# A planned one-core kernel: new costs for its planner, and 64-bit weights rounded by an integer add

## The chip, the cores and the metric

The kernel runs on one NeuronCore of a Trainium2 chip. The metric is the device time of one execution in microseconds (us). The engines are TensorE (matmuls; PE in the profile, PEld its weight loads), VectorE (DVE), ScalarE (ACT), GpSimd (POOL) and SyncE (SP), which issues nearly all DMAs. Each engine works through its own queue in order.

## The reference, cut to what matters

Three stages follow each other: a linear attention with a delta rule over 768 tokens (4 batches, 8 heads of 48), a dense block with a squared ReLU, and a dense block with a maximum over three products.

```python
for t in range(S):                                   # S = 768
    y[:, :, t] = einsum('bhd,bhde->bhe', q[:, :, t], state)
    v_old = einsum('bhde,bhd->bhe', state, kt)       # kt: k over its norm
    state = state + bt * einsum('bhd,bhe->bhde', kt, vt - v_old)
x = y.transpose(0, 2, 1, 3).reshape(B * S, H * D)    # 3072 x 384
r = maximum(x @ w_in, 0); x = (r * r) @ w_out        # 384 x 2048, 2048 x 384
h = maximum(maximum(x @ w1, x @ w2), x @ w3)         # 384 x 768 each
out = h @ w_out2                                     # 768 x 384
```

The weights arrive as 64-bit floats; the other inputs are float32.

## The kernel before, in words

The tokens are cut into 6 steps of 128 positions, each over all 4 batches (512 columns). For each step `gram` forms the products of keys with keys and queries (64x64 matmuls of `W`), `solve` inverts a triangular system of 32x32 blocks on VectorE (31 pairs of instructions, `tmp<-L,T` and `T<-T,tmp`, each needing the one before it) and finishes with 32x32 matmuls, and `chain` runs the recurrence over two chunks of 64 tokens with small matmuls (64x48 and 48x64). These matmuls are float32, and I call them small. A small matmul stands twice in the trace, each time with a weight load; a 128x128 transpose stands once.

`moe1(t)` is the first dense block of step t: 16 blocks f of 128 hidden columns; `hidden` makes 9 matmuls (three parts of x, each as high times high, high times low, low times high) and `project` 9 more. These are fp32r matmuls with 512 columns, called large here. In `moe1(0)` the blocks f = 0 to 7 run in two halves of 256 columns, so that the first half of step 0's tokens can start early. Between the two, ScalarE makes `r` and `gh`, VectorE makes `gl`. The second dense block (tiles `b0` to `b3`, `m0`, `m1`) comes last and is large matmuls alone.

`load_w` brings one 128x384 block of weights: a DMA into `raw`, ScalarE's absolute value, six VectorE instructions (a seventh, the low part, comes after ScalarE's `hi`), so that `hi + lo` is the weight rounded to float32. There are 32 loads for the first block, all inside `moe1(0)`, and 24 for the second, much later.

The order on every engine is written by the class `Planner`: all operations are recorded, each with a due place (`pl.at`, from tables such as `GRAM`, `SOLVE`, `CHAIN`) and a cost from `_Engine.record`. `forward` then plays the engines against these costs and picks, at each free engine, the ready operation with the earliest due place; on TensorE it prefers to stay with small or with large matmuls by the rules `MIX`, `FULL`, `STAY`, `BURST`, `URGENT`. `backward` sets the due places anew, and the best of 8 rounds is issued.

Of the kernel before, what the change touches and what calls it, by code (L numbers as in the profile page):

```python
# [52 lines left out]
class Planner:  # L53
# [3 lines left out]

    MIX, FULL, STAY, BURST, URGENT = 3719.33, 7024.00, 12.67, 2.43, 3.70  # L60
    INTO, BACK, RUSH = 0.09, 0.2, 0.52
    HOLD = {"vector": 0.071}
    LAG = {"tensor": 0.2, "vector": 0.13, "scalar": 0.15, "gpsimd": 0.08, "sync": 0.0}

    def __init__(self, nc):
        self.nc, self.at, self.ops, self.seen, self.joint, self.beside = nc, 0.0, [], {}, None, False
        self.free, self.first, self.end, self.before_all, self.rush = {}, 0, {}, False, False
        self.flow, self.ticks, self.start = (deque(), False, False), {}, {}
# [7 lines left out]
        yield  # L76
        self.joint, self.beside = None, False

    def add(self, engine, call, cost, outs, ins, flow, late):
        if self.joint is None or self.joint == len(self.ops):  # L80
            self.ops.append([engine, [], 0.0, set(), self.at, any(a.dtype == F32R for a in ins), 0.0, 0.0, self.before_all, self.rush])
        n = len(self.ops) - 1
        op = self.ops[n]
        op[1].append(call)
        op[2] = max(op[2], cost) + 0.007 if self.beside else op[2] + cost
# [28 lines left out]
    def forward(self, at):  # L114

        first, ops = self.first, self.ops
        free, ticks, flow, fill, big = dict(self.free), dict(self.ticks), *self.flow
        flow = deque(flow)
        left, ready, queue, seq = {}, {}, {}, []
        start, end = {}, self.end  # L120
# [13 lines left out]
        todo = len(ops) - first  # L134
        while todo:
            best = None
            for e in set(ready) | set(queue):
# [46 lines left out]
            if e == "tensor":  # L184
# [13 lines left out]
            if e == "sync":  # L198
                free[e] = t + 0.6
                free["dma"] = max(t + 1.3, free.get("dma", 0.0)) + cost  # L200
                end[n] = free["dma"] + 1.0
            else:
                free[e] = end[n] = t + cost
                if e == "scalar":
                    end[n] += ops[n][7]
# [5 lines left out]
        return seq, start, end, (free, ticks, (flow, fill, big))  # L211

    def backward(self, end):

# [13 lines left out]
        todo = len(left)  # L228
        while todo:
            best = None  # L230
            for e in set(ready) | set(queue):
                f = free.get(e, 0.0)
                if queue.get(e):
                    t = f
# [48 lines left out]
class _Engine:  # L283
# [3 lines left out]
    def __getattr__(self, what):  # L287
        fn = getattr(getattr(self.plan.nc, self.name), what)

        def record(*args, **kw):  # L290
# [5 lines left out]
            cols, late = out.free_size(), 0.0  # L296
            space = ins[0].space if ins else None
            if self.name == "tensor":
                k, m = ins[0].partition_size(), ins[0].free_size()
                if ins[0].dtype == F32R:  # L300
                    cost = cols / 2400 + 0.015
                elif what == "transpose":
                    cost = 0.11
                else:
                    cost = max(1.67 * cols, 100) / 1000
                    if m <= 32:
                        cost = 0.027
                    elif out.offset >= _row(out.tensor):
                        cost = 0.007
            elif self.name == "vector":  # L310
                fast = what in ("tensor_scalar", "tensor_copy") and space != PSUM
                cost = (cols / (2 if fast else 1) + 64) / 960
                if what == "transpose":
                    cost = (cols * 1.8 + 64) / 960
                elif what == "reciprocal":
# [1 line left out]
            elif what == "dma_start" and self.name == "scalar":  # L317
                cost, late = 0.65, 2.0
            elif self.name == "scalar":
                cost = (cols + (60 if space == PSUM else 112)) / 1200  # L320
# [9 lines left out]
            self.plan.add(self.name, lambda: fn(*args, **kw), cost, [out], ins, flow, late)  # L330

        return record

# [2 lines left out]
def kernel(  # L336
# [41 lines left out]
    GB = B // 2  # L378
    EPS = 1e-6

    GL, CL, G1, DEC, BOOST, SPL, CUT, HALF, G2, LATE, BLOCKS, FIRST, HURRY = 27, 46, -1, 97, 164, 47, 6, 8, -133, 228, 3, 2, 0
    GRAM = (0, -8, 0, 23, 17, 0)
    SOLVE = (0, 0, 0, 80, 12, -33)
    CHAIN = (-9, -8, 0, 11, -5, -19)
    TICKS = 6 * NF
    W_MIN, W_MAX = 2.0 ** -15, 122876.0

# [435 lines left out]
    def load_w(src, hi, lo, like=None):  # L823


        raw, t1, t2 = raw_ring(), xs_ring()[:, 0:DM], t2_ring()
# [4 lines left out]
        u1, u2 = t1.bitcast(U32), t2.bitcast(U32)  # L831
        pl.scalar.activation(t1, high.bitcast(F32), AF.Abs)
        pl.vector.tensor_scalar(t1, t1, W_MIN, W_MAX, op0=ALU.max, op1=ALU.min)
        pl.vector.tensor_scalar(
            u1, u1, 3, 0x3FFFFFFF, op0=ALU.logical_shift_left, op1=ALU.bitwise_and
        )
        pl.vector.scalar_tensor_tensor(
            u1, high, 0xC0000000, u1, op0=ALU.bitwise_and, op1=ALU.bitwise_or
        )
        pl.vector.tensor_scalar(u2, u1, 0xFF800000, None, op0=ALU.bitwise_and)  # L840
        pl.vector.scalar_tensor_tensor(t2, low, 2.0 ** -52, t2, op0=ALU.mult, op1=ALU.mult)
        pl.vector.tensor_tensor(t1, t1, t2, op=ALU.add)
        if like is not None:
            t1 = like(t1)
        pl.scalar.activation(hi, t1, AF.Copy)
        pl.vector.tensor_tensor(lo, t1, hi.bitcast(F32), op=sub)

    def load_in(src, f, hi, lo):
        sv = src.rearrange("(r p) f -> p r f", p=P)
# [8 lines left out]
    def moe1(t, first=0, last=NF):  # L858
# [63 lines left out]
        pl.at = at + 6 * NF + 3 - BOOST  # L922
        if t + 1 < NS:
            for o in range(KD):
                xs = xs_ring() if t + 2 < NS else x2r[1][:, o]
                if o == 1:
                    pl.vector.tensor_copy(xs, acc[o])
                else:
# [168 lines left out]
```

## Time and profile before

| | |
|---|---|
| median of 3 runs | 941.7 us (940.34 to 943.5) |
| the profiled execution | 943.03 us |
| its span in the profile | 940.6 us |
| PE busy | 868.4 us, 92% |
| DVE busy | 588.4 us, 63% |
| ACT busy | 443.1 us, 47% |

The span runs from the first to the last recorded instruction; the 2.4 us around it belong to the execution's own time. The shares are means over stages that have different limits, so the table alone does not say which engine sets the end.

### The profile page before, as it was taken

What the parts mean: (1) busy time and instruction counts of PE and PEld (TensorE: products, weight loads), DVE (VectorE), ACT (ScalarE), POOL (GpSimd) and SP (SyncE); (2) the same over time, 40 slices, a digit from 0 to 9 for tenths busy, and PEclk for the clock granted to TensorE, in tenths of its full rate; (3) what the DMA queues carried; (4) which work ended last, traced back from release to release, by engine and by line L of the source; (5) the groups of instructions that cost most, each with busy time, mean ns of one, the idle gap of its engine ahead of it and who ended that gap; (6) DMA issues with size and microseconds to landing.
All of it is one profiled execution on the core that took longest, in us unless ns stands there. A gap on an engine that the chain in (4) does not pass through costs nothing.

```text
span 940.6 us, 22413 instructions
## 1 busy us (share of the span) xinstructions
PE 868.4 (92%) x9388; PEld 731.2 (78%) x9388; DVE 588.4 (63%) x1256; ACT 443.1 (47%) x835; POOL 23.4 (2%) x33
## 2 busy tenths in 40 slices
PE   5537789999989998999999999999999999999998
PEld 4426678877877777877887888888898989898987
DVE  4999998899858957955963399883313132323221
ACT  6446458965465464555456567662212122221121
POOL 2001001000000010010000000000000000000000
PEclk9555799999999999999999999999999999999999
DMA  9744467677744746333432567670010100000000
GB/s 170 146 118 123 107 178 226 160 180 180 176 94 93 194 98 109 113 121 72 132 102 85 179 193 238 190 225 1 1 68 1 68 1 34 0 34 1 26 9 34
DMA packets 186276, 100.64 MB, mean 107 GB/s; under 512 B 150080, under 2 KB 166208, under 8 KB 186176
## 3 DMA queue, kind: packets, MB, share of 16 engines
q1 hardware_dynamic: 185328, 99.02, 40.5%
q8 instruction: 73, 1.20, 0.5%
q10 hardware_dynamic: 848, 0.20, 0.1%
q14 instruction: 27, 0.22, 0.1%
HBM read 79.53 MB, written 14.94 MB: 100 GB/s over the span
## 4 chain that ended last, share of the span: by engine, by line
PE 74%; DVE 14%; ACT 5%; DMA 3%; issue 3%; SPq 0%; DVEq 0%; ACTq 0%
PE ps L330 74%; DVE xs L330 3%; DVE T L330 2%; DVE tmp L330 2%; ACT G L330 2%; DVE t L330 2%; DVE W L330 1%; DMA raw<-in_moe_w_out_dram 1%; DMA raw<-in_moe_w_in_dram 1%; ACT r L330 1%; ACT W L330 1%; DVE gl L330 1%; ACT US L330 1%; DVE L L330 1%; ACT xs L330 0%
## 5 line engine op out<-in xcount | busy, mean ns | idle before, releaser
L330 DVE TENSOR_TENSOR r<-r,ps 128x512 f32<-128x512 f32 x72 | 49.5, 687 | 178.6 <-PE ps L330 176.6
L330 PE MATMUL ps<-gh,wo 128*128 128x512 f32 (+1 forms) x624 | 156.3, 379 | 2.8 <-ACT gh L330 2.0
L330 ACT ACTIVATE r<-ps 128x512 f32<-128x512 f32 (+1 forms) x140 | 79.9, 571 | 152.3 <-PE ps L330 142.9
L330 PEld LDWEIGHTS ps<-gh,wo 128*128 128x128 f32 x624 | 111.3, 189 | 25.2 <-ACT gh L330 2.4
L330 PE MATMUL ps<-xh,wih 128*128 128x512 f32 (+1 forms) x312 | 121.8, 390 | 2.2 <-ACT r L330 2.1
L330 PE MATMUL ps<-xh,wil 128*128 128x512 f32 (+1 forms) x312 | 117.8, 378 | 1.3 <-issue 0.9
L330 PE MATMUL ps<-xl,wih 128*128 128x512 f32 (+1 forms) x312 | 117.5, 377 | 0.0
L330 DVE TENSOR_TENSOR gl<-r,gh 128x512 fp32r<-128x512 f32 (+1 forms) x104 | 67.1, 646 | 47.2 <-ACT gh L330 45.0
L330 PE MATMUL ps<-gl,wo 128*128 128x512 f32 (+1 forms) x312 | 84.2, 378 | 2.3 <-DVE gl L330 1.3
L330 PEld LDWEIGHTS ps<-xh,wih 128*128 128x128 f32 x312 | 59.5, 191 | 15.3 <-ACT r L330 3.9
L330 PEld LDWEIGHTS ps<-xh,wil 128*128 128x128 f32 x312 | 59.7, 191 | 11.3 <-issue 1.3
L330 PEld LDWEIGHTS ps<-xl,wih 128*128 128x128 f32 x312 | 59.7, 191 | 10.6
L330 ACT ACTIVATE gh<-r 128x512 fp32r<-128x512 f32 (+1 forms) x104 | 62.1, 597 | 10.1 <-PE ps L330 7.8
L330 PEld LDWEIGHTS ps<-gl,wo 128*128 128x128 f32 x312 | 56.3, 189 | 13.5 <-DVE gl L330 1.7
L330 ACT ACTIVATE G<-ps 32x256 f32<-32x256 f32 (+3 forms) x132 | 55.4, 432 | 23.7 <-PE ps L330 21.6
L330 DVE TENSOR_TENSOR T<-T,tmp 128x31 f32<-128x31 f32 (+15 forms) x186 | 62.9, 338 | 3.5
L330 DVE TENSOR_TENSOR tmp<-L,T 128x31 f32<-128x31 f32 (+15 forms) x186 | 62.7, 337 | 3.3
L330 ACT ACTIVATE r<-r 128x512 f32<-128x512 f32 (+1 forms) x104 | 62.0, 596 | 2.4
L330 PE MATMUL ps<-W 64*64 64x64 f32 x1536 | 45.5, 246 | 14.1 <-ACT W L330 10.6
L330 PEld LDWEIGHTS ps<-W 64*64 64x64 f32 x1536 | 38.7, 156 | 21.1 <-ACT W L330 13.2
L330 DVE TENSOR_SCALAR xs<-xs 128x384 f32<-128x384 f32 x112 | 40.9, 366 | 15.0 <-ACT xs L330 14.2
L330 ACT ACTIVATE m0h<-r 128x512 fp32r<-128x512 f32 x18 | 11.4, 632 | 67.1 <-DVE r L330 67.1
(149 smaller groups left out, 1662.2 us busy)
## 6 DMA issues: line engine op xcount, KB each, us to landing
wo<-wod SPq DMA_DIRECT2D x88, 384.0 KB, 3.4
raw<-in_moe_w_out_dram SPq DMA_DIRECT2D x22, 384.0 KB, 3.6
raw<-in_moe_w_dram SPq DMA_DIRECT2D x18, 384.0 KB, 3.8
raw<-in_moe_w_in_dram SPq DMA_DIRECT2D x16, 384.0 KB, 4.2
wod<-wo SPq DMA_DIRECT2D x16, 384.0 KB, 3.7
vn<-in_v_dram SPq DMA_DIRECT2D x24, 192.0 KB, 4.4
kn<-in_k_dram SPq DMA_DIRECT2D x24, 192.0 KB, 4.8
out_dram<-ob SPq DMA_DIRECT2D x24, 192.0 KB, 1.9
```

The costliest lines, as they stand in the source:

```text
L330: self.plan.add(self.name, lambda: fn(*args, **kw), cost, [out], ins, flow, late)
```

## The change

There are three edits. First, `load_w` rounds in another way: the low word is scaled by 2^-29 on ScalarE, which leaves it as a small whole number in `raw`, and VectorE adds it as an integer to the float's bits. Two VectorE instructions fall away, the float add becomes an add on 16-bit halves (an instruction over 128x768 elements of two bytes, named `ISA` in the order below), and ScalarE has one instruction more. The tiles `xs` and `t2` give way to two `word` tiles and a third `raw` tile; the 12 stores of `x2d` go through `raw` tiles.

Second, the planner has other costs, and it counts TensorE's instructions: a boundary every 256 (`CHUNK`) may not come sooner than 3.6 us (`SUPPLY`) after the last, and when small matmuls are ahead of that by 128 (`AHEAD`), it turns to large ones. Third, all rules' numbers and due places are new; one line of each table is shown.

```diff
-    MIX, FULL, STAY, BURST, URGENT = 3719.33, 7024.00, 12.67, 2.43, 3.70
+    MIX, FULL, STAY, BURST, URGENT = 1297.88, 4709.68, 69.71, 12.05, -3.99
+    CHUNK, SUPPLY, AHEAD = 256, 3.6, 128
...
+                used = count % self.CHUNK - self.CHUNK * (t - since) / self.SUPPLY
+                thin = used > (0 if thin else self.AHEAD)
                 if None not in kinds:
-                    if fill:
+                    if fill or thin:
                         n = kinds[True][1]
...
+                over = (count + ops[n][10]) % self.CHUNK
+                if over < count % self.CHUNK:
+                    cost += max(0.0, since + self.SUPPLY - t - cost)
+                    since = t + cost
+                count += ops[n][10]
...
-    CHAIN = (-9, -8, 0, 11, -5, -19)
+    CHAIN = (-692, -620, 84, -317, 132, 232)
...
-    xs_ring = Ring(tiles(const, 2, [P, TB], F32, "xs"))
-    raw_ring = Ring(tiles(const, 2, [P, 2 * DM], U32, "raw"))
-    t2_ring = Ring(tiles(const, 2, [P, DM], F32, "t2"))
+    raw_ring = Ring(tiles(const, 3, [P, 2 * DM], U32, "raw"))
+    word_ring = Ring(tiles(const, 2, [P, DM], U32, "word"))
...
-        pl.scalar.activation(t1, high.bitcast(F32), AF.Abs)
-        pl.vector.tensor_scalar(t1, t1, W_MIN, W_MAX, op0=ALU.max, op1=ALU.min)
+        pl.scalar.activation(value, high.bitcast(F32), AF.Abs)
+        pl.vector.tensor_scalar(value, value, W_MIN, W_MAX, op0=ALU.max, op1=ALU.min)
+        pl.scalar.activation(low, low, AF.Copy, scale=2.0 ** -29)
         pl.vector.tensor_scalar(
-            u1, u1, 3, 0x3FFFFFFF, op0=ALU.logical_shift_left, op1=ALU.bitwise_and
+            word, word, 3, 0x3FFFFFFF, op0=ALU.logical_shift_left, op1=ALU.bitwise_and
         )
         pl.vector.scalar_tensor_tensor(
-            u1, high, 0xC0000000, u1, op0=ALU.bitwise_and, op1=ALU.bitwise_or
+            word, high, 0xC0000000, word, op0=ALU.bitwise_and, op1=ALU.bitwise_or
         )
-        pl.vector.tensor_scalar(u2, u1, 0xFF800000, None, op0=ALU.bitwise_and)
-        pl.vector.scalar_tensor_tensor(t2, low, 2.0 ** -52, t2, op0=ALU.mult, op1=ALU.mult)
-        pl.vector.tensor_tensor(t1, t1, t2, op=ALU.add)
+        pl.vector.tensor_tensor(word, word, low, op=ALU.add)
```

How the order moves is shown at two places. The first is VectorE in the first `solve` (step 0), at the middle of its 31 pairs. Before, the pairs (`tmp`, `T`) alternate with instructions of weight loads (`xs`, `t`, `wil`):

```order
L330 SCALAR_TENSOR_TENSOR t_85<-raw_83,t_85 128x384
L330 TENSOR_TENSOR tmp<-L,T 128x255
L330 TENSOR_TENSOR xs_81<-xs_81,t_85 128x384
L330 TENSOR_TENSOR T<-T,tmp 128x17x15
L330 SCALAR_TENSOR_TENSOR t_84<-raw_82,t_84 128x384
L330 TENSOR_TENSOR tmp<-L,T 128x256
L330 TENSOR_TENSOR wil<-xs_81,wih 128x3x128
L330 TENSOR_TENSOR T<-T,tmp 128x16x16
```

Now the same pairs stand alone there:

```order
L341 TENSOR_TENSOR tmp<-L,T 128x252
L341 TENSOR_TENSOR T<-T,tmp 128x18x14
L341 TENSOR_TENSOR tmp<-L,T 128x255
L341 TENSOR_TENSOR T<-T,tmp 128x17x15
L341 TENSOR_TENSOR tmp<-L,T 128x256
L341 TENSOR_TENSOR T<-T,tmp 128x16x16
L341 TENSOR_TENSOR tmp<-L,T 128x255
L341 TENSOR_TENSOR T<-T,tmp 128x15x17
```

The weight work that stood between the pairs has moved behind them; 22 pairs in a row, from the first, have nothing between them.

The second place is TensorE while `chain(2)` and `gram(3)` run inside `moe1(1)`, at the first chunk's update of the state (`US,kn`). `W` marks the small matmuls of `gram`, `gh,wo` and `xh,wih` large ones. Before:

```order
L330 MATMUL ps_90<-W_105 64x64
L330 MATMUL ps_88<-gh_77,wo_99 128x512 x2
L330 MATMUL ps_93<-R,G_108 64x48 x16
L330 MATMUL ps_92<-US_109,kn 48x48 x16
L330 MATMUL ps_91<-W_105 64x64
L330 MATMUL ps_90<-W_105 64x64
L330 MATMUL ps_91<-W_105 64x64
```

And now:

```order
L341 MATMUL ps_89<-W_104 64x64
L341 MATMUL ps_92<-R,G_107 64x48 x16
L341 MATMUL ps_91<-US_108,kn 48x48 x16
L341 MATMUL ps_88<-xh,wih 128x512
L341 MATMUL ps_88<-xh,wil 128x512
L341 MATMUL ps_88<-xl,wih 128x512
L341 MATMUL ps_88<-xh,wih 128x512
L341 MATMUL ps_88<-xh,wil 128x512
L341 MATMUL ps_88<-xl,wih 128x512
L341 MATMUL ps_85<-gl_78,wo_97 128x512
L341 MATMUL ps_86<-gl_78,wo_97 128x512
```

Before, 80 small matmuls follow each other here, with 2 large ones ahead of them and 3 behind. Now 16 large ones stand behind the 64 small ones that end with `US,kn`, and 18 ahead of them.

## Rows read from the trace of the kernel before

**Rows 1.** The page: busy time of the engines, and the queue that brings TensorE's instructions.

```profile
PE 868.4 (92%) x9388; PEld 731.2 (78%) x9388; DVE 588.4 (63%) x1256; ACT 443.1 (47%) x835; POOL 23.4 (2%) x33
...
q8 instruction: 73, 1.20, 0.5%
```

**Rows 2.** Busy time in stretches: start and end, length, then each engine's us (instructions).

```profile
core 0: us, PE busy (x) PEld busy (x) DVE busy (x) ACT busy (x) POOL busy (x), PEclk, DMA share, GB/s
19.00:102.00 83.00, 42.50 (x946) 35.59 (x944) 79.58 (x206) 42.27 (x88) 2.85 (x3) 0.59 0.56 131
102.00:214.60 112.60, 105.50 (x1644) 91.72 (x1640) 105.82 (x263) 79.46 (x174) 5.19 (x7) 0.97 0.65 172
214.60:518.70 304.10, 291.59 (x4709) 236.70 (x4708) 216.44 (x439) 166.73 (x296) 10.45 (x11) 0.99 0.50 120
518.70:937.00 418.30, 418.29 (x1948) 358.77 (x1944) 179.09 (x328) 143.54 (x255) 0.00 (x0) 1.00 0.23 73
...
560.00:580.00 20.00, 20.00 (x90) 16.57 (x89) 19.13 (x42) 15.48 (x29) 0.00 (x0) 1.00 0.70 224
```

**Rows 3.** TensorE in order of time: start, length, what, and the wait before it.

```profile
102.07 0.58 PE L330 MATMUL ps<-xh,wih 128*128 128x256 f32 x1
...
214.63 0.92 PE L330 MATMUL ps<-US,kn 64*48 64x48 f32 x32
...
518.73 1.65 PE L330 MATMUL ps<-gh,wo 128*128 128x512 f32 x6
```

**Rows 4.** VectorE in order of time: three marks of the first stage.

```profile
21.76 1.93 DVE L330 STREAM_TRANSPOSE L<-G 128x1024 f32<-128x1024 f32 x1 [0.42 <-ACT G L330]
...
101.48 0.42 DVE L330 TENSOR_TENSOR xl<-xr,xh 128x256 fp32r<-128x256 f32 x1
...
213.81 0.69 DVE L330 TENSOR_TENSOR gl<-r,gh 128x512 fp32r<-128x512 f32 x1
```

**Rows 5.** Groups of instructions by shape: busy us in all, mean ns of one.

```profile
L330 DVE SCALAR_TENSOR_TENSOR t<-raw,t 128x384 f32<-128x384 uint32 x56 | 31.0, 553 | 0.7
L330 ACT ACTIVATE xs<-raw 128x384 f32<-128x384 f32 x56 | 30.9, 552 | 25.5 <-DMA raw<-in_moe_w_out_dram 7.3 <-DMA raw<-in_moe_w_in_dram 4.8 <-DMA raw<-in_moe_w_dram 4.3
L330 DVE TENSOR_TENSOR xs<-xs,t 128x384 f32<-128x384 f32 x56 | 30.8, 550 | 0.6
...
L330 DVE TENSOR_SCALAR t<-xs 128x384 uint32<-128x384 uint32 x56 | 20.4, 365 | 0.6
...
L330 DVE TENSOR_TENSOR vn<-vn,nn 128x768 f32<-128x768 f32 x12 | 11.4, 953 | 1.1 <-DMA vn<-in_v_dram 1.1
```

**Rows 6.** VectorE in order of time: independent neighbours, then a chain.

```profile
70.60 0.54 DVE L330 TENSOR_TENSOR wo<-xs,wo 128x384 fp32r<-128x384 f32 x1
71.07 0.26 DVE L330 TENSOR_TENSOR T<-T,tmp 128x112 f32<-128x112 f32 x1
...
157.16 0.75 DVE L330 TENSOR_SCALAR xs<-xs 128x384 f32<-128x384 f32 x2 [0.28 <-ACT xs L330]
157.94 0.56 DVE L330 SCALAR_TENSOR_TENSOR xs<-raw,xs 128x384 uint32<-128x384 uint32 x1
```

**Rows 7.** Busy time in stretches of 64 small matmuls of `solve`, and of 12 large ones.

```profile
491.85:493.07 1.22, 1.22 (x129) 1.18 (x129) 0.60 (x1) 1.11 (x2) 0.00 (x0) 1.00 0.70 186
258.71:260.66 1.95, 1.43 (x130) 1.27 (x129) 0.00 (x0) 1.48 (x2) 0.00 (x0) 1.00 0.43 131
...
493.07:496.01 2.94, 2.94 (x20) 2.17 (x12) 1.39 (x3) 2.74 (x5) 1.90 (x2) 1.00 0.16 62
```

**Rows 8.** PEld's waits at 256 to 292, 332 to 371, 411 to 450: total, times, longest.

```profile
PEld ps L330 <- issue: 4.7, 8, 1.2
...
PEld ps L330 <- issue: 6.7, 9, 2.1
...
PEld ps L330 <- issue: 5.2, 8, 1.3
```

**Rows 9.** DMA queues from 256 to 282: packets, MB, share.

```profile
q8 instruction: 7, 0.11, 2.0%
```

More of the change, by code (lines that the diff above doesn't have):

```diff
@@ L67, in __init__ @@
         self.free, self.first, self.end, self.before_all, self.rush = {}, 0, {}, False, False
-        self.flow, self.ticks, self.start = (deque(), False, False), {}, {}
+        self.flow, self.ticks, self.start = (deque(), False, False, (0, -9.0, False)), {}, {}
         for name in ("tensor", "vector", "scalar", "gpsimd", "sync"):
@@ L77, in together, with add @@
         self.joint, self.beside = None, False
-    def add(self, engine, call, cost, outs, ins, flow, late):
+    def add(self, engine, call, cost, outs, ins, flow, late, share=0.0, count=0):
         if self.joint is None or self.joint == len(self.ops):
-            self.ops.append([engine, [], 0.0, set(), self.at, any(a.dtype == F32R for a in ins), 0.0, 0.0, self.before_all, self.rush])
+            self.ops.append([engine, [], 0.0, set(), self.at, any(a.dtype == F32R for a in ins), 0.0, 0.0, self.before_all, self.rush, 0, 0.0, 0.0])
         n = len(self.ops) - 1
@@ L84, in add @@
         op[1].append(call)
-        op[2] = max(op[2], cost) + 0.007 if self.beside else op[2] + cost
+        op[10] += count
+        op[11], op[12] = max(op[11], cost), op[12] + share
+        op[2] = max(op[11], op[12]) if self.beside else op[2] + cost
         op[6] += flow
@@ L136, in forward @@
             best = None
-            for e in set(ready) | set(queue):
+            for e in self.LAG:
                 f = free.get(e, 0.0)
@@ L203, in forward @@
                 free[e] = end[n] = t + cost
-                if e == "scalar":
-                    end[n] += ops[n][7]
+                end[n] += ops[n][7]
             todo -= 1
@@ L210, in forward @@
                     there(m)
-        return seq, start, end, (free, ticks, (flow, fill, big))
+        return seq, start, end, (free, ticks, (flow, fill, big, (count, since, thin)))
     def backward(self, end):
@@ L230, in backward @@
             best = None
-            for e in set(ready) | set(queue):
+            for e in self.LAG:
                 f = free.get(e, 0.0)
@@ L295, in record @@
                 ins.append(out)
-            cols, late = out.free_size(), 0.0
+            cols, late, share, count = out.free_size(), 0.0, 0.0, 0
             space = ins[0].space if ins else None
@@ L299, in record @@
                 k, m = ins[0].partition_size(), ins[0].free_size()
+                count = 2
                 if ins[0].dtype == F32R:
-                    cost = cols / 2400 + 0.015
+                    cost = cols / 2400 + 0.0133
                 elif what == "transpose":
@@ L304, in record @@
                 else:
[L305 to L309, printed above, removed]
+                    count = 4
+                    cost = 1.7 * cols / 1000 if m > 32 else 0.027
+                    share = cols * (1.0 if k > 64 else 0.68 if k > 32 else 0.6) / 1000
             elif self.name == "vector":
@@ L312, in record @@
                 cost = (cols / (2 if fast else 1) + 64) / 960
+                if space == PSUM or len(ins) > 1 and ins[1].space == PSUM:
+                    cost, late = cost + 0.09, -0.09
                 if what == "transpose":
@@ L319, in record @@
             elif self.name == "scalar":
-                cost = (cols + (60 if space == PSUM else 112)) / 1200
+                cost = (cols + 180) / 1160 if space == PSUM else (cols + 124) / 1200
+                late = -0.11 if space == PSUM else 0.0
             elif self.name == "gpsimd":
@@ L329, in record @@
                 flow = k * cols / 128 * (1 if ins[0].dtype == F32R or what == "transpose" else 2)
-            self.plan.add(self.name, lambda: fn(*args, **kw), cost, [out], ins, flow, late)
+            self.plan.add(self.name, lambda: fn(*args, **kw), cost, [out], ins, flow, late, share, count)
         return record
@@ L823, in load_w @@
     def load_w(src, hi, lo, like=None):
-        raw, t1, t2 = raw_ring(), xs_ring()[:, 0:DM], t2_ring()
+        raw, word = raw_ring(), word_ring()
         pl.before_all = raw_ring.n <= FIRST
@@ L830, in load_w @@
         low, high = raw[:, 0:2 * DM:2], raw[:, 1:2 * DM:2]
-        u1, u2 = t1.bitcast(U32), t2.bitcast(U32)
-        pl.scalar.activation(t1, high.bitcast(F32), AF.Abs)
-        pl.vector.tensor_scalar(t1, t1, W_MIN, W_MAX, op0=ALU.max, op1=ALU.min)
+        value = word.bitcast(F32)
+        pl.scalar.activation(value, high.bitcast(F32), AF.Abs)
+        pl.vector.tensor_scalar(value, value, W_MIN, W_MAX, op0=ALU.max, op1=ALU.min)
+        pl.scalar.activation(low, low, AF.Copy, scale=2.0 ** -29)
         pl.vector.tensor_scalar(
-            u1, u1, 3, 0x3FFFFFFF, op0=ALU.logical_shift_left, op1=ALU.bitwise_and
+            word, word, 3, 0x3FFFFFFF, op0=ALU.logical_shift_left, op1=ALU.bitwise_and
         )
         pl.vector.scalar_tensor_tensor(
-            u1, high, 0xC0000000, u1, op0=ALU.bitwise_and, op1=ALU.bitwise_or
+            word, high, 0xC0000000, word, op0=ALU.bitwise_and, op1=ALU.bitwise_or
         )
-        pl.vector.tensor_scalar(u2, u1, 0xFF800000, None, op0=ALU.bitwise_and)
-        pl.vector.scalar_tensor_tensor(t2, low, 2.0 ** -52, t2, op0=ALU.mult, op1=ALU.mult)
-        pl.vector.tensor_tensor(t1, t1, t2, op=ALU.add)
+        pl.vector.tensor_tensor(word, word, low, op=ALU.add)
         if like is not None:
-            t1 = like(t1)
-        pl.scalar.activation(hi, t1, AF.Copy)
-        pl.vector.tensor_tensor(lo, t1, hi.bitcast(F32), op=sub)
+            value = like(value)
+        pl.scalar.activation(hi, value, AF.Copy)
+        pl.vector.tensor_tensor(lo, value, hi.bitcast(F32), op=sub)
     def load_in(src, f, hi, lo):
@@ L924, in moe1 @@
             for o in range(KD):
-                xs = xs_ring() if t + 2 < NS else x2r[1][:, o]
+                xs = raw_ring()[:, 0:TB].bitcast(F32) if t + 2 < NS else x2r[1][:, o]
                 if o == 1:
```

12 lines of the change are left out of this document (6 added, 6 removed).

## The prediction

> **What bounds the kernel now.** I read the busy time by stretches first. The reader is to see four stages there [rows 2]. [...] From 214.6 to 518.7 TensorE is busy 291.6 of 304.1 us and VectorE only 216. From 518.7 on TensorE is busy 418.29 of 418.30 us and everything else has room. So an end can come earlier only by what TensorE finishes sooner before 518.7.
>
> The marks between the stages come from the order of time [rows 3]. The first large matmul starts at 102.07. At 214.63 the 432nd is done: all 288 half-width ones of the first step and 144 of full width. At 518.73 the last small matmul is done, with 1332 large ones issued; I counted these places in the written order and found their rows. Behind that stand 1944 large matmuls without a gap. A full-width one costs 20/90 = 0.222 us [rows 2], in the last line.
>
> In the first two stages VectorE sets the pace. Its marks are the start of the first `solve` at 21.76, the first `xl` at 101.48, which the first large matmul needs, and the 24th `gl` at 213.81, the last of step 0, which stands at the same place as TensorE's 214.63 [rows 4].
>
> In the third stage the wait to look at is "issue", in which TensorE waits for nothing that the profile shows. The same 64 small matmuls of `solve` take 1.22 us in one place and 1.95 in another, where TensorE is busy for 1.43 only [rows 7]. The two engine rows hold 18,776 instructions, and the instruction queue brought 73 packets, so one packet serves 257 [rows 1]. From 256 to 282 us seven came, one in 3.7 us [rows 9]. A small matmul is four instructions (two records, each with a weight load), so 64 of them use up a packet in 1.22 us. A large one is two instructions in 0.222 us, a packet in 28 us. In dense stretches of small matmuls the instructions therefore come too slowly. In the three rounds where `gram` and `chain` meet, the weight loads wait 4.7, 6.7 and 5.2 us for "issue" [rows 8].
>
> **The weight loads.** Each load loses one `TENSOR_SCALAR` (0.365) and one `SCALAR_TENSOR_TENSOR` (0.553) on VectorE [rows 5], 0.92 us. The float add (0.550) becomes the 16-bit add, which the trace does not show. Its lower bound is 0.365, like a single-source instruction on as many words; its upper bound is 0.953, that of `vn`, which takes 768 elements one by one. I take 0.55: the instruction writes as many bytes as the float add, which is the nearest row. [...]
>
> ScalarE's extra instruction is like `xs<-raw`, 0.552 [rows 5]. It can run as soon as the absolute value is out, beside two `TENSOR_SCALAR` and a `SCALAR_TENSOR_TENSOR` of VectorE, so I cost it at nothing. If that cover went, VectorE would wait in its queue up to 0.55 per load, with `gl` and the `solve` pairs behind it. ScalarE in the second stage would rise from 79.5 of 112.6 us by 21 x 0.552 to about 91 of 107. The third `raw` tile only loosens the DMAs. The `x2d` stores take `raw` tiles when no weights are loading, so nothing waits for them.
>
> **VectorE's new order.** Independent neighbours overlap by 0.07 to 0.08 us: 0.54 long, but the next starts 0.47 later. A chain does not: two of 0.36 take 0.75 and the next starts at 0.78, which is 0.03 lost at each step [rows 6]. Between the first and the second mark stand 199 instructions before, 89.2 us of durations, 10 of them chained. With the overlaps this makes 89.2 - 189 x 0.08 + 10 x 0.03 = 74.4, against 79.7 in the trace, so 5.3 us were idle. The changed order has 167 instructions there, because weight work moved behind the bare `solve` pairs and each load lost two: 74.7 us of durations with the traced means, 66 chained. This makes 74.7 - 101 x 0.08 + 66 x 0.03 = 68.6. With the same idle time the first large matmul comes 5.8 us sooner, at about 96.
>
> Between the second and third mark stand 262 instructions before (122.7 us, 23 chained: 104.3, and 8 idle). Now there are 241 (113.7 us, 36 chained: 98.4). That is 5.9 us more. So the 432nd large matmul should come 11.7 us sooner, near 203. TensorE can follow: its 432 large ones need 288 x 0.111 + 144 x 0.222 = 64 us; its remaining small ones, 1.2 thousand records at an estimated 0.02, need 24; 20 change-overs at 0.27 (12 large ones took 2.94 in place of 2.67 [rows 7]) need 5. That is 93 of 107 us.
>
> **TensorE's new order in the third stage.** Of the 16.6 us of "issue", 25 waits at the 0.27 of a change-over would be 6.8 with no shortage at all. So 9.8 is the least that is lost to supply and 16.6 the most; I take 13. In the second and third rounds no run of small matmuls is now longer than 64, and 15 to 18 large ones stand between most of them: such a pair of runs uses about 290 instructions in 2.0 + 3.6 us, slower than one packet in 3.7. I expect nearly all of the loss there back. In the first round a run of 96 stays, and I expect half. That is 11 of 13. Against it stand 46 runs of large matmuls in place of 41, 5 x 0.27 = 1.4 us. Nine large matmuls move behind the last small one, which shifts 2.0 us between the stages and costs nothing. The other rules and due places act only through this order.
>
> **The sum.** 11.7 + 11 - 1.4 = 21.3 us. The profiled execution took 943.0, so the same execution would take 921.7. It stood 1.3 above the median of 941.7, so I forecast a median of 920.5, say **921 us**. A difference of 0.3% (2.8 us) is about what a measurement of this kernel can tell from no change.
>
> **The rivals.** (a) *The add runs one half-word per cycle.* At 0.953 each of the 29 loads between the first and third mark gives 0.40 back, 11.7 us. The first stages then gain nothing, the third stays: 932 us. For it speaks that the only 768-element row takes 0.953; against it, that the bytes are the float add's. Chance 0.12.
>
> (b) *Instruction supply is not what costs.* Then the "issue" waits are change-overs, which the new order has five more of, and only VectorE's 11.7 us come: 941.7 - 11.7 + 1.4 = 931 us. Against it speak the equal sets of matmuls at 1.22 and 1.95 us, and the packet every 3.7 us. [...] Chance 0.08.
>
> (c) *TensorE takes over as the bound of the second stage.* If the small matmuls cost more than 0.02 a record at the lower clock, TensorE gives back VectorE's gain, and only the third stage counts: 941.7 - 9.6 = 932 us. The point is 107 - 93 = 14 us of unforeseen work. Chance 0.08.
>
> (d) *Slower: the integer add waits for ScalarE.* The low word now comes from ScalarE's queue, in which a ReLU or a square (about 0.6 each) may stand ahead. The wait blocks VectorE's whole queue and with it `gl`, for which TensorE waits. With 29 loads before the third mark, 21.3 / 29 = 0.73 us a load is the point from which the kernel is slower. A copy behind one other instruction would cost 1.15 at worst, 33 us in all: 953 us. Against it speaks the cover of three VectorE instructions; for it, a ScalarE that is 85% busy there. Chance 0.12.
>
> **The numbers.** My forecast has a chance of 0.60, with its own range of 912 to 930: at the low end an add of 0.365 (5 us) and all 16.6 us of supply, at the high end half of either gain. (a), (b) and (c) end at 931 to 932, so the range of 8 in 10 goes from 909 to 936. Faster by over 0.3%: 0.60 + 0.12 + 0.08 + 0.08, of which I keep 0.87. Slower is (d), at 0.11, and 0.02 is left for no change.
>
> **What would show it.** The 16-bit add at about 0.55 us; the first large matmul near 96 and the 432nd near 203; VectorE's time between 20 and 200 still over 90% busy; the three rounds with "issue" waits of about 2 us each; the last small matmul near 497; 420 us of large matmuls behind it, unchanged in rate. The prediction is wrong if the add stands at 0.95, if VectorE waits for ScalarE at `word`, if the rounds still show "issue" waits of 5 us, or if the granted clock stays at the lower level in stretches where it was at the upper one.

## The result and the profile after

The changed kernel takes 918.75 us (median of 4 runs, 917.18 to 919.55), against 942.11 us (940.34 to 943.5) for the kernel before beside it: a ratio of 0.975, 95% interval 0.973 to 0.977. The forecast was 921 in a range of 909 to 936. The profiled execution went from 943.03 us to 918.45.

The page after, with the lines that answer to [rows 1]:

```profile
PE 862.6 (94%) x9388; PEld 727.0 (79%) x9388; DVE 558.0 (61%) x1144; ACT 466.0 (51%) x891; POOL 23.3 (3%) x33
...
q8 instruction: 73, 1.20, 0.6%
```

VectorE has 112 instructions less and ScalarE 56 more, two and one for each of 56 loads. TensorE has the same number of instructions in the same number of packets. The stretches that answer to [rows 2], cut at the same places in the work:

```profile
19.00:96.40 77.40, 42.99 (x1026) 36.78 (x1022) 71.40 (x175) 46.91 (x100) 2.84 (x3) 0.66 0.62 132
96.40:206.50 110.10, 104.98 (x1641) 89.98 (x1638) 100.75 (x237) 88.43 (x195) 5.18 (x7) 0.97 0.66 177
206.50:492.00 285.50, 283.96 (x4636) 231.06 (x4634) 219.00 (x436) 164.85 (x292) 10.46 (x11) 1.00 0.54 126
492.00:912.40 420.40, 420.31 (x1957) 360.65 (x1953) 160.96 (x280) 154.48 (x283) 0.00 (x0) 1.00 0.23 74
```

The first stage ends 5.6 us sooner. The second is 2.5 us shorter (112.6 to 110.1) and the third 18.6 (304.1 to 285.5). The third also holds fewer matmuls: nine large ones and 64 records of small ones have left it. Those small ones now run in the first stage; the second holds about as many as before (1172 for 1176). In the third TensorE's own idle time falls from 12.5 us (304.10 - 291.59) to 1.5. The last stage is 2.1 longer, the nine large matmuls that moved behind the last small one. TensorE's marks, as in [rows 3]:

```profile
96.44 0.58 PE L341 MATMUL ps<-xh,wih 128*128 128x256 f32 x1
...
206.15 0.50 PE L341 MATMUL ps<-xl,wih 128*128 128x512 f32 x1
...
492.02 0.50 PE L341 MATMUL ps<-xh,wih 128*128 128x512 f32 x1
```

These are the first large matmul, the 432nd, and the first large one behind the last small one. The new instructions, by shape, as in [rows 5]:

```profile
L341 DVE CUSTOM_DVE_ANT_0 word<-raw,word 128x768 uint16<-128x768 uint16 x56 | 30.9, 554 | 3.2 <-ACT raw L341 1.0
...
L341 ACT ACTIVATE raw<-raw 128x384 uint32<-128x384 uint32 x56 | 30.4, 551 | 8.9 <-DMA raw<-in_moe_w_in_dram 5.5 <-issue 1.8 <-DMA raw<-in_moe_w_out_dram 1.0
```

The 16-bit add takes 0.554 us, the 0.55 that the sum used. Ahead of it VectorE stood idle for 3.2 us in all, 1.0 of it waiting for ScalarE's copy.

Last, the waits that answer to [rows 8]: the weight loads' waits for "issue" in the three rounds of `gram` and `chain` (241 to 275, 317 to 352, 395 to 428):

```profile
PEld ps L341 <- issue: 4.0, 8, 1.5
...
PEld ps L341 <- issue: 1.8, 5, 0.4
...
PEld ps L341 <- issue: 1.4, 4, 0.4
```

And TensorE's own waits for it over the whole third stage, before and after:

```profile
PE ps L330 <- issue: 9.8, 10, 1.9
```
```profile
PE ps L341 <- issue: 1.4, 1, 1.4
```

All 9.8 us of before lie in the three rounds (256 to 292, 332 to 371, 411 to 450), and the 1.4 of after in the first of them:

```profile
PE ps L330 <- issue: 2.5, 3, 1.0
...
PE ps L330 <- issue: 4.1, 3, 1.9
...
PE ps L330 <- issue: 3.2, 4, 1.2
```

### The profile page after: what moved, and what is told of

It reads as the page before. It is cut to its first block, busy times and chain, and to the rows that moved or that the text cites. A ratio compares the mean times of both kernels' runs of the same rounds, so it can differ in the third digit from the quotient of the medians.

```text
span 915.9 us, 22310 instructions
## 1 busy us (share of the span) xinstructions
PE 862.6 (94%) x9388; PEld 727.0 (79%) x9388; DVE 558.0 (61%) x1144; ACT 466.0 (51%) x891; POOL 23.3 (3%) x33
## 4 chain that ended last, share of the span: by engine, by line
PE 84%; DVE 7%; ACT 4%; issue 2%; DMA 1%; SPq 1%; DVEq 0%; ACTq 0%
PE ps L341 84%; DVE word L341 2%; SPq L341 1%; DVE T L341 1%; DVE tmp L341 1%; ACT G L341 1%; DMA xr<-Y 1%; DVE W L341 1%; ACT word L341 1%; DMA raw<-in_moe_w_in_dram 0%; DVE US L341 0%; ACT W L341 0%; ACT r L341 0%; DVE st L341 0%; DVE G L341 0%
## 5 line engine op out<-in xcount | busy, mean ns | idle before, releaser
L341 PEld LDWEIGHTS ps<-gh,wo 128*128 128x128 f32 x624 | 110.1, 189 | 20.3
L341 DVE TENSOR_SCALAR word<-word 128x384 f32<-128x384 f32 (+1 forms) x112 | 41.7, 375 | 15.9 <-ACT word L341 14.4
L341 PEld LDWEIGHTS ps<-W 64*64 64x64 f32 x1536 | 35.0, 152 | 16.2 <-ACT W L341 11.0
L341 PE MATMUL ps<-W 64*64 64x64 f32 x1536 | 40.0, 240 | 7.8 <-ACT W L341 7.6
```

## Experiments

Two theories were tested for the first two stages. V: VectorE sets the pace. T: TensorE bounds the second stage, rival (c) of the prediction. D is that ScalarE's extra copy costs, as in rival (d). For the third stage, S is the short supply of instructions, B that it is hidden. In E1 to E4 and E8 the planner plays with the costs of its own kernel and only then other instructions are put in place of those it planned, so the order on TensorE, VectorE, ScalarE and SyncE stays as it was but for the instructions named:

```diff
-            self.plan.add(self.name, lambda: fn(*args, **kw), cost, [out], ins, flow, late, share, count)
+            call, self.plan.swap = self.plan.swap or (lambda: fn(*args, **kw)), None
+            self.plan.add(self.name, call, cost, [out], ins, flow, late, share, count)
```

In the traces of the kernel before and of the changed one, VectorE, ScalarE and TensorE start their work in the order in which it is written: all 1256 and 1144 instructions of VectorE, all 834 and 890 of ScalarE on tiles, and in each all 3276 large matmuls.

The kernel before was run beside all of them: median 940.46 us for E1 to E4, 939.91 for E5 to E8, 939.95 for E9 to E12.

### E1: the old rounding in the new order

```diff
+        pl.swap = lambda: None
         pl.scalar.activation(low, low, AF.Copy, scale=2.0 ** -29)
...
+        def old():
+            lowf, highf = low.bitcast(F32), high.bitcast(F32)
+            nc.vector.tensor_scalar(high, word, 0xFF800000, None, op0=ALU.bitwise_and)
+            nc.vector.scalar_tensor_tensor(lowf, low, 2.0 ** -52, highf, op0=ALU.mult, op1=ALU.mult)
+            nc.vector.tensor_tensor(value0, value0, lowf, op=ALU.add)
+        value0, pl.swap = value, old
         pl.vector.tensor_tensor(word, word, low, op=ALU.add)
```

> The changed kernel's order on every engine, written out as it is, but each weight load rounds as before the change: VectorE has the TENSOR_SCALAR and the SCALAR_TENSOR_TENSOR again (0.365 + 0.553, some 0.76 us a load after the overlaps) and ScalarE's extra copy is gone. 8 loads lie between the first and the second mark of VectorE, 21 between the second and the third. Theory V (VectorE sets the pace in both stages): 29 x 0.76 = 22 us more, about 941, the time before the change. Rival T (TensorE bounds the second stage, where VectorE now has 9 us idle): 8 x 0.76 = 6 in the first stage and 16 - 9 = 7 in the second, about 932. If the rounding is worth nothing and the order everything: within 3 us of 919. The third stage should keep its length (286 us from the 432nd large matmul to the last small one) in all three.

Measured: 957.11 us, 38 more than the changed kernel and slower than before (ratio 1.016, 1.011 to 1.021). Its stretches:

```profile
19.00:104.50 85.50, 43.39 (x1053) 37.38 (x1053) 80.12 (x194) 43.23 (x92) 2.95 (x3) 0.66 0.58 120
104.50:227.00 122.50, 108.19 (x1639) 91.55 (x1638) 118.79 (x279) 81.12 (x176) 5.29 (x7) 0.96 0.60 161
227.00:514.50 287.50, 285.28 (x4636) 231.80 (x4634) 218.92 (x436) 164.87 (x292) 10.47 (x11) 0.99 0.55 125
514.50:952.60 438.10, 427.86 (x1957) 358.49 (x1953) 181.89 (x328) 145.35 (x258) 0.00 (x0) 1.00 0.22 71
```

The first two stages grow by 8.1 and 12.4, together 20.5 of the 22 that V gave, with VectorE at 118.79 of 122.5 us. The third keeps its length. None of the theories had the last stage: 438.1 in place of 420.4 us for the same 1953 large matmuls. The 24 loads of the second block lie there, and TensorE waits 9.3 us in it for `r`, `gh` and `gl`. The order of before does the same loads with the old rounding in a last stage of 418.3 us, so it is this order that leaves them no more room than the new rounding needs.

### E2: the new rounding in the old order

```diff
+        def new():
+            nc.scalar.activation(a1, high.bitcast(F32), AF.Abs)
+            nc.scalar.activation(low, low, AF.Copy, scale=2.0 ** -29)
+        a1, pl.swap = t1, new
         pl.scalar.activation(t1, high.bitcast(F32), AF.Abs)
...
+        pl.swap = lambda: None
         pl.vector.tensor_scalar(u2, u1, 0xFF800000, None, op0=ALU.bitwise_and)
+        pl.swap = lambda: nc.vector.tensor_tensor(u1, u1, low, op=ALU.add)
         pl.vector.scalar_tensor_tensor(t2, low, 2.0 ** -52, t2, op0=ALU.mult, op1=ALU.mult)
+        pl.swap = lambda: None
         pl.vector.tensor_tensor(t1, t1, t2, op=ALU.add)
```

> The order of the kernel before on every engine, with the new rounding in its place: the integer add stands where the SCALAR_TENSOR_TENSOR stood, the float add and one TENSOR_SCALAR are gone, ScalarE's copy stands right behind its absolute value; two raw tiles. 11 loads lie between the first and second mark, 17 between the second and third. Theory V: 28 x 0.76 = 21 us less, about 921, all of it ahead of the 432nd large matmul, and the third stage still 304 us with weight loads waiting 4.7, 6.7 and 5.2 us for issue. Rival T: 8 us in the first stage and at most the 7 us that TensorE was idle in the second, about 927. If the rounding is worth nothing without the new order: within 3 us of 942.

Measured: 938.13 us, ratio 0.9965 (0.9943 to 0.9988). The stretches:

```profile
19.00:100.20 81.20, 42.01 (x941) 35.40 (x940) 73.02 (x183) 47.03 (x99) 2.85 (x3) 0.58 0.58 135
100.20:213.00 112.80, 105.84 (x1644) 91.64 (x1644) 94.64 (x229) 87.28 (x192) 4.93 (x7) 0.97 0.66 172
213.00:512.40 299.40, 289.08 (x4709) 235.52 (x4709) 215.04 (x436) 166.90 (x296) 10.45 (x11) 1.00 0.51 122
```

The first stage is only 1.8 us shorter, where V and T both gave it 8. Between its first two marks VectorE has 8.6 us less of durations, but 4.0 us more of idle time, and its instructions overlap by 2.8 us less. In the second stage VectorE loses 11 us of work (105.82 to 94.64) and the stage stays at 112.8. Two waits of VectorE in that stage show where part of that went, first before, then in E2:

```profile
DVE wil L330 <- ACT wih L330: 2.9, 3, 1.1
DVE xs L330 <- ACT xs L330: 1.5, 4, 0.6
```
```profile
DVE xs L331 <- ACT xs L835: 4.8, 8, 1.4
DVE wil L331 <- ACT wih L331: 4.6, 4, 1.6
```

So V's 921 fails here, and T's 927 does too. What holds is the third rival, that the rounding is worth nothing, within 3 us, without the new order: it is 2.3 us below the median beside it. In the old order less work on VectorE doesn't shorten the second stage, in which TensorE is busy for 105.8 of 112.8 us and VectorE now waits for ScalarE, and even the first stage keeps most of its length.

### E3, E4, E8: VectorE and ScalarE lightened or loaded at a fixed order

E3 leaves the integer add out, E4 the copy, E8 does the copy twice (the line is what stands in place of the planned one):

```diff
+        pl.swap = lambda: None                                                       # E3: the add
+        pl.swap = lambda: None                                                       # E4: the copy
+        pl.swap = lambda: nc.vector.tensor_tensor(word, word, zero, op=ALU.add)      # E4: the add
+        nc.scalar.activation(low, low, AF.Copy)                                      # E8: behind the copy
```

> The changed kernel's order, with the integer add left out (the weights stay truncated). VectorE loses 0.47 us a load after the overlap. Theory V: 29 x 0.47 = 13.7 us less, about 905. Rival T: only the first stage's 8 x 0.47 = 3.8 us, about 915. Together with the run with the old rounding this gives the slope on both sides.

> The changed kernel's order, with ScalarE's extra copy left out; the integer add adds a tile of zeros instead of the low word, so that its low part is missing from the weights. My costing (the copy is hidden behind VectorE's work): no change, 917 to 920. Rival D (VectorE, or the squares on ScalarE that TensorE waits for, come late because of it): up to 0.55 a load, 29 x 0.55 = 16 us less at the most, 903; anything over 3 us speaks for it.

> The changed kernel's order, with ScalarE's extra copy done twice (the second changes no value). It shows how near ScalarE is to the path: by my costing the cover of three VectorE instructions is 0.35 + 0.35 + 0.55 us less overlaps, about 1.1 us, and two copies take 1.1, so 919 to 923. Rival D: ScalarE, 88 of 110 us busy in the second stage, becomes its bound and each of the 21 loads there costs up to 0.55, up to 12 us more, 931.

Measured: E3 911.53 us, E4 915.17, E8 928.56; against 918.75 that is -7.2, -3.6 and +9.8. The first two stages of E3:

```profile
19.00:92.70 73.70, 42.76 (x1009) 37.22 (x1009) 66.38 (x164) 44.89 (x96) 2.84 (x3) 0.63 0.61 137
92.70:199.70 107.00, 103.62 (x1639) 89.13 (x1638) 92.36 (x216) 88.16 (x196) 5.29 (x7) 0.98 0.67 183
```

The first stage gains 3.7, just what V and T gave it. The second loses 8.4 us of VectorE's work and gains 3.1, between T's nothing and V's 9.9. One place shows why: the longest run of large matmuls in that stage, 276 in a row, in the changed kernel, in E3, in E4 and in E1:

```profile
105.46:143.31 37.85, 36.29 (x280) 34.60 (x276) 35.90 (x93) 30.74 (x75) 0.97 (x1) 1.00 0.70 226
```
```profile
100.71:138.47 37.76, 36.34 (x280) 34.64 (x276) 33.76 (x86) 30.81 (x76) 0.97 (x1) 1.00 0.68 226
```
```profile
103.34:141.17 37.83, 36.47 (x280) 34.66 (x277) 36.54 (x95) 28.27 (x67) 0.96 (x1) 1.00 0.69 227
```
```profile
112.77:157.23 44.46, 39.00 (x280) 36.34 (x277) 43.53 (x111) 28.05 (x68) 0.97 (x1) 0.96 0.60 196
```

Neither less VectorE nor less ScalarE shortens it, and more VectorE lengthens it at once. In this run the changed kernel stands at the point where the two bounds meet. E4 and E8 show that ScalarE's copy isn't free: the 432nd large matmul ends at 206.65 in the changed kernel, at 203.98 in E4 and at 211.65 in E8. Behind that mark E4 gains nothing; E8 loses 6 us more in the last stage (426.5 for 420.4). Set against the kernel before beside each, E4's gain is 2.6 us rather than 3.6, and the two intervals overlap (ratios 0.968 to 0.976, 0.973 to 0.977), so its size is known only roughly; E8's loss is well clear of noise. My costing of the copy (917 to 920 for E4, 919 to 923 for E8) is out in both.

### E5: the supply by itself

```diff
+        for gap in (15, 6, 0):
+            large(90)
+            for i in range(8):
+                small(i)      # 64 matmuls 32x32 on ident, as in solve
+                large(gap)
+        large(90)
```

> The changed kernel with three series behind its last matmul, each after 90 large ones: 8 sets of 64 small 32x32 matmuls of the form of solve, with 15, then 6, then no large ones behind each set. It adds work, the outputs are as before. Theory S (instructions come at one packet of 257 in 3.7 us): a set with 15 large ones needs 286 instructions in 1.22 + 3.6 = 4.8 us and loses nothing; with 6 it needs 268 in 2.8 us, so it takes 3.9; bare sets need 256 each and take 3.7, apart from the first one or two, which are there already. So the series take about 39, 29 to 31 and 25 to 30 us. Rival B (supply is hidden, only change-overs cost): 39, 22 and 10 us.

This kernel was timed once, at 1096.02 us; what counts are its stretches. Of the series with 15 large ones the second set, alone and with its large ones; of that with 6 the fourth, likewise; the first bare set; all eight bare ones:

```profile
938.02:939.23 1.21, 1.21 (x129) 1.17 (x128) 0.00 (x0) 0.00 (x0) 0.00 (x0) 1.00 0.07 14
938.02:942.86 4.84, 4.84 (x144) 3.91 (x143) 0.00 (x0) 0.00 (x0) 0.00 (x0) 1.00 0.02 3
1003.56:1005.78 2.22, 1.43 (x130) 1.27 (x129) 0.00 (x0) 0.00 (x0) 0.00 (x0) 1.00 0.00 0
1003.56:1007.36 3.80, 3.01 (x135) 2.32 (x135) 0.00 (x0) 0.00 (x0) 0.00 (x0) 1.00 0.02 4
1042.96:1044.05 1.09, 1.09 (x129) 1.09 (x132) 0.00 (x0) 0.00 (x0) 0.00 (x0) 1.00 0.00 0
1042.96:1070.34 27.38, 13.69 (x1026) 12.71 (x1025) 0.00 (x0) 0.00 (x0) 0.00 (x0) 0.62 0.02 4
```

S holds in all three: 4.84 us where there is time (seven of the eight sets lose nothing, one takes 0.7 us longer), 3.80 where 2.8 would do, and (27.38 - 1.09) / 7 = 3.76 us for a bare set of 256 instructions. B's 10 us for the bare series are 27.4. TensorE alone is busy in them, and the instruction queue of [rows 1] brings seven packets:

```profile
q8 instruction: 7, 0.11, 1.8%
```

That is one for each of the seven sets of 3.76 us.

### E6, E7, E11: which part of the planner does it

E6 is the changed kernel without the counting, E7 the kernel before with the counting alone, E11 the changed kernel with all due places of before:

```diff
-    CHUNK, SUPPLY, AHEAD = 256, 3.6, 128
+    CHUNK, SUPPLY, AHEAD = 256, 1e-9, 1e9
...
-    CHAIN = (-692, -620, 84, -317, 132, 232)
+    CHAIN = (-9, -8, 0, 11, -5, -19)
```

> The changed kernel with the counting of TensorE's instructions taken out of the planner (no boundary costs anything, no turn to large matmuls on its account); all other costs, rules and due places as changed. The order of all engines is planned anew. Theory S: the runs of small matmuls in the third stage grow again and its length from the 432nd large matmul to the last small one goes from 286 towards 298 us, so 924 to 930. Rival (the due places alone spread the small matmuls): third stage within 3 us of 286, time within 3 us of 919.

> The kernel before with the counting alone added to its planner (256, 3.6, 128); its other costs, rules, due places and rounding as before. Theory S: the third stage, 304 us, falls by 5 to 11 us, the first two stay, so 931 to 937. Rival (without due places that leave room, the counting only delays small matmuls on which large ones depend): no gain or a loss, 940 or more.

> The changed kernel with the due places of the kernel before (GL to HURRY, GRAM, SOLVE, CHAIN); costs, counting, rules' numbers and rounding as changed. If the due places spread the small matmuls (the run without counting kept the third stage's gain): waits for issue in the third stage rise again to 5 us or more and it takes 295 us or more, 928 to 945. If the costs and rules do it: 283 to 290 us and 915 to 925.

Measured: E6 914.23 us (ratio 0.972, 0.969 to 0.975), E7 955.77 (1.016, 1.013 to 1.020), E11 930.74 (0.990, 0.986 to 0.993). The third stage of E6, E7 and E11 (that of E7 with 58 more large matmuls than before, that of E6 with 12 fewer than after):

```profile
203.20:485.50 282.30, 280.55 (x4624) 228.55 (x4622) 218.41 (x433) 162.56 (x290) 10.47 (x11) 1.00 0.54 125
```
```profile
224.30:538.50 314.20, 303.44 (x4768) 246.60 (x4767) 222.65 (x454) 171.25 (x303) 10.47 (x11) 1.00 0.49 117
```
```profile
219.80:505.70 285.90, 281.96 (x4636) 232.19 (x4636) 216.16 (x424) 164.29 (x292) 10.45 (x11) 1.00 0.52 121
```

Without the counting the third stage keeps its gain (282.3 + 12 x 0.22 = 285.0), and with the old due places too. TensorE's waits for "issue" in it are 1.6 and 2.3 us. So either may go by itself; what E6 and E11 share, and E9 with the old rounding too, are the new costs and the numbers of the rules, which were not run alone. S's forecast for E6, a longer third stage and 924 to 930 us, is out: without the counting the kernel is no slower. With the counting alone (E7) 58 large ones account for 12.9 of its 314.2 us: 301.3, a gain of 3, while its second stage takes 124.4; so its rival, a loss, came true. The due places earn theirs in the second stage: 124.6 us in E11 against 110.1. TensorE waits there 9.9 us for ScalarE's `r`, and its granted clock is 0.91 in place of 0.97, which may have a share in the 124.6. So E11's time misses the 915 to 925 that went with the short third stage.

### E9, E10: each part of the change by itself, planned anew

E9 has the planner and the due places as changed with `load_w` and its tiles as before; E10 has the new `load_w` and its tiles with the planner and the due places of before.

> The planner's part of the change alone, planned anew: costs, counting, rules and due places as changed, the rounding, the tiles and the stores of x2d as before. In the fixed order the old rounding took 38 us more than the changed kernel, of which 20 in the first two stages and 18 behind the last small matmul. Theory V (VectorE's work itself is the cost): the planner knows the longer loads, but 29 x 0.76 = 22 us of VectorE stay ahead of the 432nd large matmul, so 935 to 945. Rival O (the loss is in an order that was made for other durations): 920 to 928. In both the third stage keeps 283 to 290 us and TensorE's waits for issue there stay below 3 us.

> The rounding's part of the change alone, planned anew: the new rounding, its tiles and the third raw tile, with the costs, rules and due places of the kernel before. In the fixed order it was worth 2 to 3 us. Theory V: with an order that knows the shorter loads VectorE's 21 us come out ahead of the 432nd large matmul, 921 to 930. Rival T (TensorE has no room in the first two stages, its order must change for that): 934 to 942. In both the third stage keeps 299 to 305 us and its 8 to 10 us of TensorE's waits for issue.

Measured: E9 939.94 us (ratio 1.000, 0.998 to 1.001), E10 935.48 (0.996, 0.994 to 0.998). Stages two and three of E9, then of E10:

```profile
102.40:224.30 121.90, 110.76 (x1654) 95.54 (x1651) 112.65 (x276) 84.33 (x181) 4.82 (x7) 0.92 0.66 175
224.30:508.90 284.60, 281.99 (x4652) 228.75 (x4652) 218.54 (x437) 160.53 (x286) 10.45 (x11) 1.00 0.52 120
```
```profile
98.90:218.60 119.70, 110.34 (x1756) 94.88 (x1754) 104.97 (x251) 89.13 (x195) 4.88 (x7) 0.97 0.68 174
218.60:509.90 291.30, 285.03 (x4633) 232.06 (x4631) 206.50 (x416) 164.88 (x291) 10.44 (x11) 0.99 0.49 116
```

E9 has the short third stage, and loses much of it ahead: its first two stages are 9.4 us longer than before. E10 has a first large matmul 3.1 us sooner and a second stage that is longer, some of it for 112 more small records (48 from the first stage, 64 from the third). Theory V's 935 to 945 holds for E9, rival T's 934 to 942 for E10. E10's third stage misses what both theories gave it: 291.3 us in place of 299 to 305, and 4.0 us of TensorE's waits for "issue" in place of 8 to 10, with the planner and due places of before. Apart the two parts give 0 and 0.4%, together 2.5%. Neither half was given rules' numbers and due places of its own, so what each would be worth in an order made for it stays open.

For the third stage all kernels can be set side by side, with the matmuls that moved out of it or into it counted back (0.222 us a large one, 0.92 for 32 small records):

| kernel | third stage, us | TensorE's waits for "issue", us |
|---|---|---|
| before | 304.1 | 9.8 |
| E2, the same order | 299.4 | 7.8 |
| E7, before with the counting | 301.3 | 4.8 |
| E10, planned anew by the old planner | 295.8 | 4.0 |
| E9 | 290.8 | 2.4 |
| E11 | 289.7 | 2.3 |
| changed | 289.3 | 1.4 |
| E6 | 288.8 | 1.6 |

The four with the new costs and rules' numbers stand within 2 us of each other. The four without them differ by 8 us among themselves, and in E10 8.3 of the changed kernel's 14.8 us came with the planner's costs and rules of before. So the new costs and rules are shown to give the short third stage each time, but not to be the only way to most of it.

### E12: a candidate

```diff
-        pl.scalar.activation(low, low, AF.Copy, scale=2.0 ** -29)
+        pl.gpsimd.tensor_scalar(low, low, 2.0 ** -29, None, op0=ALU.mult)
```

> A candidate from the runs so far: the changed kernel without the counting (914.2) and with the extra scaling moved from ScalarE to GpSimd, which is busy for 23 us only. Leaving the copy out gave 3.6 us at a fixed order. Theory V and T both: 911 to 914 if GpSimd does 128x384 in about 1 us beside VectorE. Rival: GpSimd takes far longer than ScalarE's 0.55 (its affine work on this many elements has no row here), VectorE waits for it at the integer add, 915 or more; at 1.5 us over the cover of 1.1 it costs up to 29 x 0.4 = 12 us.

Measured: 927.49 us, 13.3 more than E6, so the rival is right. GpSimd needs 1.4 us for the scaling, and it costs more than ScalarE's copy. Part of the loss may be the order, since the planner reckons with 384 x 2.2 / 960 + 0.1 = 0.98 us for it; that was not tested apart:

```profile
L341 POOL TENSOR_SCALAR raw<-raw 128x384 uint32<-128x384 uint32 x56 | 78.1, 1395 | 222.7 <-DMA raw<-in_moe_w_in_dram 74.7 <-DMA raw<-in_moe_w_dram 62.1 <-DMA raw<-in_moe_w_out_dram 40.0
```

E6 has the lowest median of the kernels that compute the whole reference. It was not timed beside the changed kernel, and the two intervals (0.969 to 0.975, 0.973 to 0.977) overlap, so it isn't shown to be faster.

## Why the prediction was right, and where its terms were off

**The weight loads: right.** The add takes 0.554 us for 768 two-byte elements, and the bound of 0.953, the time of 768 float ones [rows 5] (rival (a)), is out. In the first stage of the new order a load's work on VectorE is worth its duration: E3 takes 8 x 0.47 = 3.8 from it and it ends 3.8 sooner (92.66 against 96.44).

**The first stage: right.** 5.8 us forecast, 5.6 measured. VectorE did a little better than the sum: 72.3 us between its first two marks, where I had 73.9 and before had 79.7. Of these 7.4 us 0.5 were lost by a later start (22.28 for 21.76) and 1.3 at the end, where the first large matmul now starts 1.9 us behind the first `xl` instead of 0.6, after a wait of 1.05 us of TensorE's small matmuls for ScalarE's `US`. E2 shows that this gain belongs to the new order: in the old one the same rounding gave 1.8 us.

**The second stage: the term was too large.** I forecast 5.9 us and TensorE's 432nd near 203; it ends at 206.65, 2.5 us of gain in the stage. The step that failed is "TensorE can follow", with 93 of 107 us: TensorE is busy for 105. The row for it stood among those of before, 105.5 us busy for nearly the same matmuls [rows 2], and my prices should have been held against it. The 276 large ones alone take 37.85 us, where my prices give 258 x 0.111 + 18 x 0.222 = 32.6; a half-width one follows the last after 0.120 us and not after half of 0.222. Over the whole stage the stretches of large matmuls take 78.8 us with their waits, where I had 64, and those of small ones 31.3, which is 0.027 for each of 1172 records, where I had 24, at an estimated 0.02, and 5 for change-overs. So rival (c)'s mechanism is there, at a price of a few us and not of all 11.7. The lower clock that it names, 0.50, holds in the first 6 us of the stage (102 to 108 before, 96.4 to 102 after); behind that it is 0.99 and 1.00.

**ScalarE's copy at nothing: too low.** It costs about 3 us (2.6 to 3.6 by E4's median, 2.7 by the mark). Rival (d) had the sign, but hardly the place: VectorE waited for the copy at the add for 1.0 us in all. It did not come near its point of 0.73 us a load. By which of ScalarE's later instructions the rest reaches TensorE was not taken apart.

**The third stage: right in mechanism, too small.** Net of the nine large ones, which only move, it is 18.6 - 2.0 = 16.6 us shorter; I had 11 - 1.4. TensorE's waits for "issue" give 8.4 of it, less than my 11. Its other waits give 2.6, and 1.8 comes from the 64 small records that now run in the first stage, where TensorE has room. The remaining 3.8 is busy time, where I expected change-overs to add 1.4; which matmul records became shorter was not taken further apart. The weight loads' "issue" waits of the second and third round, 1.8 and 1.4, are as forecast; the first round kept 4.0 of its 4.7, where I expected half back. E5 shows the supply itself. E2 has TensorE's order of before, 7.8 us of its "issue" waits and a stage of 299.4 us, so this loss is no fixed sum of an order.

**The last stage: right**, 420.4 us. That it stays so is no matter of course: with the old rounding in this order it takes 438 (E1).

**What the sum did not say.** It added VectorE's gain and the supply's as two terms that stand by themselves. In the changed kernel both come, but not as priced: 8.1 us of the 11.7 ahead of the 432nd large matmul, and 16.6 behind it where I had 9.6. That 921 stands so near to 918.75 is in part luck, because the two misses cancel. Made one at a time the two parts don't add up: the planner's part alone gains 13 us in the third stage (19.5, less 5.3 for 24 large ones and 0.9 for 32 small records that lie elsewhere), gives 9.4 back ahead of it (its 432nd large matmul ends at 224.07, that of before at 214.70) and has the median of before (E9; the 4 us that are left are the two profiled executions, 3.1 us above and 1.3 below these medians), and the rounding's part alone has orders in which less work on VectorE doesn't shorten the second stage (E2, E10). And the counting, which the change names, is not needed for the gain (E6).

## What to carry to other kernels

Where a planner writes the order, a faster operation and the order made for its duration are one change: time both halves alone and together before you credit either. Runs of small matmuls have a price beside their execution time: here 256 instructions, 64 small float32 matmuls, need 3.75 us, so put some 15 large matmuls behind each such set. Before you count an engine's idle time as your gain, read the next engine's busy time from rows of the same stage; here it was 105 of 110 us, and a sum of single prices gave 93.

## What the runs showed of the hardware that was not expected

In E5's bare series TensorE is busy for half of the time. Its granted clock is 1.00 at the start and 0.50 soon after, and the bare sets still take about 3.75 us each: from 1049 to 1070 us, at 0.50 to 0.55, 712 records run, 128 in 3.78 us. With one packet for each bare set, the packets and not the clock set this pace:

```profile
1043.00:1049.00 6.00, 3.19 (x337) 2.96 (x337) 0.00 (x0) 0.00 (x0) 0.00 (x0) 1.00 0.02 5
...
1056.00:1063.00 7.00, 3.65 (x258) 3.38 (x252) 0.00 (x0) 0.00 (x0) 0.00 (x0) 0.50 0.02 5
```

In E12 VectorE's shift and mask takes longer beside GpSimd's scaling, 466 ns in the mean for 377, the changed kernel first:

```profile
L341 DVE TENSOR_SCALAR word<-word 128x384 uint32<-128x384 uint32 x56 | 21.0, 377 | 1.0
```
```profile
L341 DVE TENSOR_SCALAR word<-word 128x384 uint32<-128x384 uint32 x56 | 26.0, 466 | 1.1
```

In E12 the 31 of these instructions that no scaling of GpSimd overlaps take 344 to 362 ns, and of the 25 that one overlaps 20 take 568 to 1068. What in the scaling holds them up is not shown. In the changed kernel 54 of the 56 take 343 to 364.
